# Windowed attention into a top-1 mixture of experts: the last routing groups, the row scale of the last two chunks and the early slices behind attention, put in another order and partly on another engine

## The chip, the cores and the metric

One core of one Trainium2 chip. The metric is the device time of one execution in microseconds (us), start to end. Engines: TensorE (PE, matmuls), VectorE (DVE), ScalarE (ACT), GpSimd (POOL), SyncE (SP, which here only issues DMA transfers). About 0.3% (2.0 us) is what a measurement of this kernel can tell from no change.

## The reference

Eight batches of eight heads, 576 positions of 64 numbers, causal attention in a window of 128 with a linear bias; then each of the 4,608 rows of 512 numbers goes to the one expert (of eight) with the largest logit.

```
scores = where(mask, q @ k.T / 8 + bias, -1e9)          # mask: 0 <= i - j < 128
attn = softmax(scores);  x = (attn @ v) as rows [4608, 512]
logits = x @ w_gate                                     # [4608, 8]
e = argmax(logits, 1);  g = softmax(logits)[e]
out[row] = g * (relu(x[row] @ w1[e]) @ w2[e])           # w1: 512x1024, w2: 1024x512
```

## The kernel before

**Attention** runs over 36 chunks of 128 rows, four steps for each, 152 steps in all. Through step 151 the order of every engine is the order in which the code is written. A chunk ends in `rows`: four pairs of matmuls (L206) form the 128 rows and their logits in the accumulation tile `r_ps`, of which there is one; VectorE takes the reciprocal of the softmax sum (L203) and multiplies by it (L211), first the 16 columns with the logits, then the 128 with the rows, into `x_sb`; `done` then sums the logits (`lg`, L1145) and issues the store of the rows to `xd` in HBM on SyncE's queue (L1152).

**Routing** (`route`, L404 to L470) runs over groups of chunks, `GROUPS`; a generator whose pieces are taken at the steps that `PACE` names. Its pieces: (a) `mx`, `sh`, `key`, `mk`, `oh`, `prev`: which expert each row has; (b) matmuls of `oh` with triangles (L421 to L425) in a tile borrowed from `r_ps` or from the early slices' tiles, and from it `pick`, the gates (`put_gates`, L488 to L496: the gate is written into a column of the same rows in `xd`, so its DMA must land behind the row's store), the running counts, `rank`, `t`; (c) `p`, `lp`, `c`, `big`; (d) `c`, `c`, `eq`, `rr`; (e) matmuls of `lp` with `rr` (L468), which are added to `base` (L470). `base` becomes the list of rows of each expert. The very last chunk, 35, has a short form, `route_last` (L500 to L553): its one-hot rows `l_oh`, its rank matmuls (L521), `l_rr`, four tiles `l_lp` (L542), eight small matmuls (L545), and `idx`, the list by which GpSimd gathers the rows of the first expert (`xg`, L589); the gather waits for all stores and gates.

**Early slices.** Expert 0's first 256 rows are known before attention ends. `moe_early` gathers them, transposes them in two tiles (matmuls at L598, `e_xh` on ScalarE, then `e_xl` on VectorE) and computes seven slices of the first layer on them, "0" to "6": twelve matmuls each (L637; the last four read `e_xl`), then `e_hh` on ScalarE (L640) and `e_hl` on VectorE (L641). `EP` names the steps of slices 0 to 2, and `LE` what `route_last` puts between its own parts ("3", "4", "5" and "6", nothing). `st["warm"](n)` runs entry n of `LE`, and each entry beyond the last slice lets matmuls of the second layer run: `y_ps` (L820), which need `e_hh` and `e_hl`; the first of them also needs the tile in which (e) of the last full group stood, so it waits for L470. Weights and inputs are split in a high and a low part, so every product is three matmuls.

The last full group before is that of chunks 30 to 34, its pieces (a) and (b) at steps 149 and 150 and the rest in `route_last`; the one ahead of it has chunks 27 to 29.

Of the kernel before, what the change touches and what calls it, by code (L numbers as in the profile page):

```python
# [36 lines left out]
def attention(ctx, tc, st, qT, kT, v, c1, cb, iw, load_c2, chunk_done, chunks, begun):  # L37
# [1081 lines left out]
def attn_moe_kernel(ctx, tc, qT, kT, v, c1, cb, c2, iw, w12, out):  # L1119
# [9 lines left out]
    with ExitStack() as actx:  # L1129
# [9 lines left out]
        def done(ch, subs, x_sb):  # L1139
# [7 lines left out]
            for lo in (0, 2):  # L1147
                if lo == 2 and subs[0][0] == subs[2][0]:
                    continue
                n = 64 if subs[0][0] != subs[2][0] else 128  # L1150
                t0 = subs[lo][0] * S + QB * subs[lo][1]
                nc.sync.dma_start(out=st["xd"][t0:t0 + n].rearrange("t (p x) -> t p x", p=NP),  # L1152
                                  in_=x_sb[QB * lo:QB * lo + n, :, 0:SUB])
# [67 lines left out]
```

## Time and profile before

| | |
|---|---|
| median of 3 runs | 672.38 us (671.96 to 673.99) |
| profiled execution | 670.84 us |
| its span | 669.1 us, so 1.7 us lie outside |
| PE / DVE / ACT / POOL busy | 645.0 / 397.8 / 315.3 / 311.7 us |

The change touches what runs between 217 and 256 us of the span: the end of attention, and the passage to the second layer of expert 0. Of each row of the trace one reads when an instruction began, how long it took, and, in square brackets, how long its engine had stood idle and what it then waited for. A row with a count stands for several instructions that follow each other.

### The profile page before, as it was taken

The page shows a single profiled execution, that of the slowest core. Times are in us where ns is not written, and L with a number is a line of the kernel's source. Part 1 is how long each engine was busy: PE and PEld are TensorE (multiplying, and loading weights), DVE is VectorE, ACT ScalarE, POOL GpSimd, SP SyncE. Part 2 cuts the span into 40 slices and gives each one's busy share as a digit, 9 for nine tenths or more (in the row PEclk, how much of TensorE's full clock was granted, in tenths as well). Part 3 has the DMA queues.
Part 4 walks back from the last instruction along what each step waited for, and adds up shares of the span by engine and source line. Part 5 has one row for each costly group of instructions (what it writes and reads, how often), then busy time and mean ns, then how long its engine had stood idle before and what let it go on. Part 6 is the DMA issues. An engine that isn't in the chain of part 4 may idle for free.

```text
span 669.1 us, 15750 instructions
## 1 busy us (share of the span) xinstructions
PE 645.0 (96%) x5985; PEld 546.8 (82%) x5985; DVE 397.8 (59%) x984; ACT 315.3 (47%) x957; POOL 311.7 (47%) x420
## 2 busy tenths in 40 slices
PE   8899999999999989999999999999999999999995
PEld 3587787887787878889888989898898989888884
DVE  3468878887888877554564465455456455456411
ACT  3677787888787521442343334233333333333311
POOL 2556466786764504016525742860762560471202
PEclk9999999999999999999999999999999999999998
DMA  8676797795862416428344433533542533454201
GB/s 316 200 199 175 182 235 174 241 260 151 259 160 65 97 50 190 126 111 273 106 146 151 132 100 110 163 101 97 168 125 84 183 105 82 157 145 110 91 1 58
DMA packets 57488, 98.43 MB, mean 147 GB/s; under 512 B 11701, under 2 KB 31413, under 8 KB 56514
## 3 DMA queue, kind: packets, MB, share of 16 engines
q1 hardware_dynamic: 48994, 77.38, 39.4%
q0 software_dynamic: 8416, 20.02, 10.5%
q8 instruction: 48, 0.79, 0.5%
q14 instruction: 30, 0.25, 0.1%
HBM read 78.40 MB, written 18.98 MB: 146 GB/s over the span
## 4 chain that ended last, share of the span: by engine, by line
PE 51%; issue 9%; POOL 4%; DVE 1%; DMA 1%; ACT 1%; POOLq 0%; ACTq 0%
PE y_ps L820 24%; PE l_ps L637 24%; POOL xg L617 2%; POOL out L808 1%; PE s_ps L637 1%; PE x_ps L598 1%; PE x_ps L196 1%; PE y_ps L780 1%; DMA xg<-xd,idx 0%; PE r_ps L206 0%; DMA xd<-x_sb 0%; DVE x_sb L211 0%; PE x_ps L780 0%; ACT pe L159 0%; POOLq L872 0%
## 5 line engine op out<-in xcount | busy, mean ns | idle before, releaser
L640 ACT ACTIVATE hh<-l_ps 128x336 fp32r<-128x336 f32 (+7 forms) x104 | 46.4, 447 | 203.4 <-PE l_ps L637 203.1
L641 DVE SCALAR_TENSOR_TENSOR hl<-l_ps,hh 128x336 fp32r<-128x336 f32 (+7 forms) x104 | 52.1, 502 | 150.2 <-ACT hh L640 150.1
L617 POOL DMA_INDIRECT xg<-xd,od_idx x112 | 118.1, 1054 | 36.9 <-issue 36.2
L159 ACT ACTIVATE pe<-s_ps,nmax 128x128 f32<-128x128 f32 x288 | 102.2, 371 | 48.9 <-DVE nmax L155 39.5
L820 PE MATMUL y_ps<-wh,hh 128*128 128x512 f32 (+5 forms) x280 | 110.9, 396 | 0.0
L820 PE MATMUL y_ps<-wh,hl 128*128 128x512 f32 (+5 forms) x280 | 110.4, 394 | 0.0
L820 PE MATMUL y_ps<-wl,hh 128*128 128x512 f32 (+5 forms) x280 | 110.3, 394 | 0.0
L808 POOL DMA_INDIRECT out<-y,od_pidx x33 | 34.8, 1055 | 149.3 <-ACT y L826 143.1
L912 DVE TENSOR_TENSOR wl<-w_raw,wh 128x512 fp32r<-128x512 f32 x114 | 73.8, 689 | 32.9 <-ACT wh L908 30.8
L637 PE MATMUL l_ps<-xh,wh 128*128 128x304 f32 (+9 forms) x416 | 81.7, 318 | 0.0
L637 PE MATMUL l_ps<-xh,wl 128*128 128x304 f32 (+9 forms) x416 | 81.0, 317 | 0.0
L637 PE MATMUL l_ps<-xl,wh 128*128 128x304 f32 (+9 forms) x416 | 80.8, 316 | 0.0
L637 PEld LDWEIGHTS l_ps<-xh,wh 128*128 128x128 f32 x416 | 68.1, 189 | 8.4 <-issue 1.2
L637 PEld LDWEIGHTS l_ps<-xh,wl 128*128 128x128 f32 x416 | 66.4, 189 | 1.9
L637 PEld LDWEIGHTS l_ps<-xl,wh 128*128 128x128 f32 x416 | 66.3, 189 | 1.7
L196 PE MATMUL x_ps<-pT,v_sb 128*64 128x128 f32 (+2 forms) x1152 | 66.3, 265 | 0.1
L196 PEld LDWEIGHTS x_ps<-pT,v_sb 128*64 128x64 f32 (+1 forms) x1152 | 57.0, 137 | 7.9 <-issue 2.8
L820 PEld LDWEIGHTS y_ps<-wh,hl 128*128 128x128 f32 (+5 forms) x280 | 51.4, 184 | 13.6
L908 ACT CAST wh<-w_raw 128x1024 fp32r<-128x1024 f32 x57 | 59.5, 1044 | 5.5 <-DMA w_raw<-w 5.5
L820 PEld LDWEIGHTS y_ps<-wl,hh 128*128 128x128 f32 (+5 forms) x280 | 51.6, 184 | 11.3
L159 ACT ACTIVATION_READ_ACCUMULATOR pe<-s_ps,nmax 128x1 f32 x288 | 60.2, 209 | 0.0
L138 PE MATMUL s_ps<-k_sb,q_sb 64*64 64x192 f32 (+2 forms) x1152 | 58.3, 311 | 1.9 <-DMA k_sb<-kT 1.9
(211 smaller groups left out, 972.6 us busy)
## 6 DMA issues: line engine op xcount, KB each, us to landing
w_raw<-w SPq DMA_DIRECT2D x64, 512.0 KB, 3.9
q_sb<-qT SPq DMA_DIRECT2D x40, 256.0 KB, 6.4
xd<-x_sb SPq DMA_DIRECT2D x32, 258.0 KB, 4.8
v_sb<-v SPq DMA_DIRECT2D x32, 256.0 KB, 5.2
k_sb<-kT SPq DMA_DIRECT2D x7, 1152.0 KB, 8.5
w_n<-w SPq DMA_DIRECT2D x4, 1024.0 KB, 8.0
xg<-xd,od_idx POOLq DMA_INDIRECT x112, 2.9
xd<-x_sb SPq DMA_DIRECT2D x8, 129.0 KB, 4.8
```

What stands on the lines that cost most here:

```text
L138: nc.tensor.matmul(out=s_ps[halves(a), c, n, x0:x1], lhsT=blocks["q", b, m][h, 2 * g + n, qs], rhs=batch[b][h, 2 * g + n, k0:k0 + x1 - x0] ...
L159: nc.scalar.activation(out=pe[:, h, :], in_=s_ps[:, c, n, lo:lo + 128], func=AF.Exp, bias=nmax[:, 2 * c + n:2 * c + n + 1], scale=1.0, acc ...
L196: nc.tensor.matmul(out=x_ps[64 * c:64 * c + 64, p, q], lhsT=blocks["v", b, m - 1 + kb][0:kk, D * h:D * h + D], rhs=pT[0:kk, kb, h, q], sta ...
L598: nc.tensor.transpose(out=x_ps[:, d, :], in_=g[:, SUB * d:SUB * d + 128], identity=st["ident"])
L617: ins = tc.nc.gpsimd.indirect_dma_start(out=g[:, s], out_offset=None, in_=parts, in_offset=bass.IndirectOffsetOnAxis(ap=idx[:, s], axis=0),)
L637: nc.tensor.matmul(out=ps, lhsT=a[:, 128 * d:128 * d + 128], rhs=b[:, d], start=(k == 0), stop=(k == 11))
L640: nc.scalar.activation(out=hh, in_=ps, func=AF.Relu)
L641: nc.vector.scalar_tensor_tensor(out=hl, in0=ps, scalar=0.0, in1=hh.bitcast(F32), op0=ALU.max, op1=ALU.subtract)
L808: ins = nc.gpsimd.indirect_dma_start(**kw).ins
L820: nc.tensor.matmul(out=ys[t][0:n], lhsT=a[:, tl], rhs=b[:, 512:1024], start=(f == 0 and k == 0), stop=(f == 7 and k == 2))
L908: keep(tc, nc.scalar.copy(out=wh, in_=raw))
L912: keep(tc, eng.tensor_tensor(out=wl[:, sl], in0=raw[:, sl], in1=wh.bitcast(F32)[:, sl], op=ALU.subtract))
```

## The change

- The last full groups are cut anew: chunks 27 to 31 (five), then 32 to 34 (three). The pieces of the five are at steps 142, 144, 145, 146 and 148, in place of those of 27 to 29 at 138, 142, 144, 146 and 148. Pieces (a) and (b) of the three are at steps 149 and 150.
- In the last full group the cuts between the pieces lie elsewhere: `t`, `p`, `lp` are one piece, taken ahead of slices 5 and 6; gates, `c`, `big`, `c`, `c`, `eq`, `rr` are the next one, taken behind slices 5 and 6. The first half of its `rr` goes to GpSimd.
- For chunks 34 and 35 the long half of the row scale (128 columns) is no longer one operation of VectorE but eight of ScalarE, one for each head, each with its column of `rinv` as scale. They and the row's store are put off: for 34 behind the piece of step 149, for 35 behind `l_pick` in `route_last`.
- Slices 1 and 2 stand at step 149 one behind the other, each in a tile of its own; before, 2 was at step 150, behind the rank matmuls of the group. In `route_last` slice 3 has its matmuls where they were, and its `e_hh` and `e_hl` stand behind `l_pick`.
- The four `l_lp` are made ahead of slice 4, and the eight matmuls that use them (L545 before) stand in a row ahead of the first matmul of the second layer, not among those.

```
-PACE = {21: (122, 126, 130, 132, 134), 27: (138, 142, 144, 146, 148), 30: (149, 150)}
-GROUPS = ((0, 5), (5, 5), (10, 5), (15, 6), (21, 6), (27, 3), (30, 5), (35, 1))
+PACE = {21: (122, 126, 130, 132, 134), 27: (142, 144, 145, 146, 148), 32: (149, 150)}
+GROUPS = ((0, 5), (5, 5), (10, 5), (15, 6), (21, 6), (27, 5), (32, 3), (35, 1))
...
-EP = {60: "z", 134: "g", 143: "p0", 146: "p1", 147: "0", 149: "1", 150: "2"}
+EP = {60: ("z",), 134: ("g",), 143: ("p0",), 146: ("p1",), 147: "0", 149: "12"}
...
+        def scale_heads():
+            for h in range(H):
+                cols = slice(D * (h % 2), D * (h % 2) + D)
+                nc.scalar.activation(out=x_sb[:, h // 2, cols], in_=r_ps[:, h // 2, cols], func=AF.Copy, scale=rinv[:, h:h + 1])
+
+        scale(128, E)
+        if ch < N // 128 - 2:
+            scale(0, D)
+        chunk_done(ch, subs, x_sb, scale_heads)
...
+    final = c0 + G == N // 128 - 1
...
+    if final:
+        yield
+        gates()
     c = rp.tile([128, G], F32, name="c")
...
-        nc.vector.tensor_tensor(out=rr[:, :, k, :], in0=eq,
+        eng = nc.gpsimd if final and k == 0 else nc.vector
+        eng.tensor_tensor(out=rr[:, :, k, :], in0=eq,
...
+    for evict in st.pop("later"):
+        evict()
+    st.pop("store")()
     put_gates(tc, st, gate, groups)
-    st["warm"](2)
+    t0 = EARLY // 128
+    lps = {}
+    for t in range(t0, TT):
+        lps[t] = rp.tile([128, 128], BF16, name=f"l_lp{t}", bufs=1)
+        nc.vector.tensor_scalar(out=lps[t], in0=st["i128"], scalar1=s, scalar2=-128.0 * t, op0=ALU.subtract,
+                                op1=ALU.is_equal)
+    for n in (1, 2, 3):
+        st["warm"](n)
+        for r in st["rest"]:
+            if n < 3:
+                next(r)
     for r in st["rest"]:
         list(r)
...
-    st["warm"](3)
...
+            if ch < N // 128 - 2:
+                store()
+            else:
+                st["store"] = lambda: (scale(), store())
```

Of what moves, three places. First VectorE between the two `e_xl`, near the end of attention. Before, piece (b) of the group of three is over when the first `e_xl` comes, and (c) and (d) stand around the `x_sb` of chunk 32 (line numbers are those of each kernel):

```order
L438 TENSOR_SCALAR t<-t 128x3
L601 TENSOR_TENSOR e_xl<-s_ps,e_xh 128x4x128
L602 COPY e_gate<-e_xg 128x1
L446 SCALAR_TENSOR_TENSOR p<-t,rank 128x3
L448 TENSOR_TENSOR lp<-c_sb,p 128x384
L451 TENSOR_SCALAR c<-mk 128x3
L453 TENSOR_SCALAR big<-rank 128x3
L203 RECIPROCAL rinv<-rsum 128x8
L211 TENSOR_TENSOR x_sb<-r_ps,rinv 128x4x16
L211 TENSOR_TENSOR x_sb<-r_ps,rinv 128x4x128
L1145 TENSOR_REDUCE lg<-x_sb 128x8
L455 TENSOR_TENSOR c<-c,t 128x3
```

and now piece (b) of the group of five stands behind the first `e_xl`, ahead of that `x_sb`,

```order
L632 TENSOR_TENSOR e_xl<-s_ps,e_xh 128x4x128
L633 COPY e_gate<-e_xg 128x1
L439 TENSOR_TENSOR pick<-r_ps,oh 128x40
L444 TENSOR_REDUCE gate<-ex 128x5
L517 TENSOR_SCALAR gate<-gate 128x5
L519 RECIPROCAL gate_4279<-gate 128x5
L450 TENSOR_REDUCE run<-oh 128x8
L451 TENSOR_TENSOR run<-run 128x8
L453 TENSOR_REDUCE rank<-pick 128x5
L457 TENSOR_SCALAR t<-rank 128x5
L458 TENSOR_SCALAR t<-t 128x5
L203 RECIPROCAL rinv<-rsum 128x8
```

with (c) and (d) of the five in one piece ahead of the second `e_xl`:

```order
L467 SCALAR_TENSOR_TENSOR p<-t,rank 128x5
L469 TENSOR_TENSOR lp<-c_sb,p 128x640
L475 TENSOR_SCALAR c<-mk 128x5
L477 TENSOR_SCALAR big<-rank 128x5
L480 TENSOR_TENSOR c<-c,t 128x5
L481 TENSOR_TENSOR c<-c,big 128x5
L483 TENSOR_TENSOR eq<-c_sb,c 128x240
L488 TENSOR_TENSOR rr<-eq,c_sb 128x5x48 x2
L632 TENSOR_TENSOR e_xl<-s_ps,e_xh 128x4x128
```

So `pick`, which frees the `r_ps` that the matmuls of chunk 32 take, moved behind `e_xl`, and the second `e_xl` behind the whole of a longer block.

Second, VectorE from the `e_hl` of slice 5 on. Before, (c) and (d) of the last full group are over by then, and only `base` follows the last `e_hl`:

```order
L641 SCALAR_TENSOR_TENSOR e_hl<-s_ps,e_hh 128x256
L529 TENSOR_SCALAR l_rr<-l_oh,c_sb 128x8 x2
L532 ISA l_pick,rank<-x_ps,l_oh 128x8
L532 ISA rank 128x1
L491 TENSOR_SCALAR l_gate<-l_gate 128x1
L493 RECIPROCAL gate_4574<-l_gate 128x1
L641 SCALAR_TENSOR_TENSOR e_hl<-s_ps,e_hh 128x256 x2
L470 TENSOR_TENSOR base<-base,t_ps 128x48
```

Now the two `e_hl` of slices 5 and 6 come first, and gates, `c`, `big`, `eq` and VectorE's half of `rr` stand between them and `base`:

```order
L674 SCALAR_TENSOR_TENSOR e_hl<-s_ps,e_hh 128x256 x2
L444 TENSOR_REDUCE gate<-ex 128x3
L517 TENSOR_SCALAR gate<-gate 128x3
L519 RECIPROCAL gate_4623<-gate 128x3
L475 TENSOR_SCALAR c<-mk 128x3
L477 TENSOR_SCALAR big<-rank 128x3
L480 TENSOR_TENSOR c<-c,t 128x3
L481 TENSOR_TENSOR c<-c,big 128x3
L483 TENSOR_TENSOR eq<-c_sb,c 128x144
L488 TENSOR_TENSOR rr<-eq,c_sb 128x3x48
L496 TENSOR_TENSOR base<-base,t_ps 128x48
```

Nine operations moved behind the last slice; the four `l_lp` that stood behind `base` are gone from there.

Third, ScalarE between the `e_hh` of slice 0 and that of slice 6. Before:

```order
L640 ACTIVATE e_hh<-s_ps 128x256
L239 COPY xT<-x_ps 128x512
L411 ACTIVATE ex<-sh 128x40
L640 ACTIVATE e_hh<-s_ps 128x256 x2
L515 ACTIVATE l_ex,l_gate<-lg,l_mx 128x8
L640 ACTIVATE e_hh<-s_ps 128x256
L1033 COPY sel<-c_sb 128x512
L640 ACTIVATE e_hh<-s_ps 128x256 x3
```

Now, with the eight scales of chunk 34 ahead of the `e_hh` of slices 1 and 2, and those of chunk 35 between the ones of slices 3 and 4:

```order
L673 ACTIVATE e_hh<-s_ps 128x256
L249 COPY xT<-x_ps 128x512
L423 ACTIVATE ex<-sh 128x24
L219 ACTIVATE x_sb<-r_ps,rinv 128x64 x8
L673 ACTIVATE e_hh<-s_ps 128x256 x2
L541 ACTIVATE l_ex,l_gate<-lg,l_mx 128x8
L673 ACTIVATE e_hh<-s_ps 128x256
L219 ACTIVATE x_sb<-r_ps,rinv 128x64 x8
L673 ACTIVATE e_hh<-s_ps 128x256
L1068 COPY sel<-c_sb 128x512
L673 ACTIVATE e_hh<-s_ps 128x256 x2
```

The `e_hh` of slices 1 and 2 moved behind eight scales, that of slice 4 behind another eight.

## Rows read from the trace of the kernel before

**Rows 1.** The view that cuts the span into stretches, around the passage to the second layer: start and end of the stretch and its length, busy time of each engine with its instructions in brackets, granted clock of TensorE, share of the DMA engines, GB/s.

```profile
238.00:244.00 6.00, 4.98 (x45) 4.87 (x45) 4.93 (x27) 1.67 (x6) 0.00 (x0) 1.00 0.23 49
244.00:250.00 6.00, 4.56 (x44) 4.22 (x42) 4.54 (x21) 1.19 (x4) 0.00 (x0) 1.00 0.17 46
250.00:256.00 6.00, 5.81 (x33) 4.12 (x33) 3.75 (x28) 0.22 (x1) 2.86 (x3) 1.00 0.34 89
256.00:292.00 36.00, 36.00 (x232) 31.72 (x231) 23.11 (x66) 13.78 (x31) 6.03 (x6) 1.00 0.53 169
```

**Rows 2.** The timeline of TensorE's matmuls from 222 to 256 us: start, duration, engine, line, operation, out<-in, shape, count, and in square brackets the idle time ahead of it with what ended it.

```profile
225.63 1.15 PE L206 MATMUL r_ps<-iw_sb,xT 128*128 128x144 f32 x8
227.22 0.65 PE L168 MATMUL t_ps<-c_sb,pe 128*128 128x128 f32 x4 [0.44 <-ACT pT L170]
...
232.80 1.97 PE L196 MATMUL x_ps<-pT,v_sb 128*64 128x128 f32 x32
...
238.36 0.18 PE L421 MATMUL t_ps<-oh,tri 128*128 128x40 bf16 x1 [0.84 <-DVE oh L415]
...
240.07 1.14 PE L206 MATMUL r_ps<-iw_sb,xT 128*128 128x144 f32 x8
...
243.29 0.17 PE L521 MATMUL x_ps<-l_oh,tri 128*128 128x8 bf16 x1 [0.66 <-DVE l_oh L517]
...
247.00 0.75 PE L637 MATMUL s_ps<-e_xh,wh 128*128 128x256 f32 x4 [0.57 <-DVE e_hl L641]
...
248.55 0.42 PE L468 MATMUL t_ps<-rr,lp 128*128 128x48 bf16 x10
249.84 0.47 PE L820 MATMUL y_ps<-wh,e_hh 128*128 128x512 f32 x1 [0.87 <-DVE base L470]
...
251.34 0.39 PE L820 MATMUL y_ps<-wl,e_hh 128*128 128x512 f32 x1
...
255.04 0.66 PE L598 MATMUL x_ps<-c_sb,xg 128*128 128x128 f32 x4 [0.19 <-DMA xg<-xd,idx]
```

**Rows 3.** The timeline of VectorE over the same place, columns as in the group ahead.

```profile
226.72 0.69 DVE L601 TENSOR_TENSOR e_xl<-s_ps,e_xh 128x512 fp32r<-128x512 f32 x1 [1.17 <-ACT e_xh L600]
...
227.38 0.50 DVE L446 SCALAR_TENSOR_TENSOR p<-t,rank 128x3 f32<-128x3 f32 x1
227.92 0.56 DVE L448 TENSOR_TENSOR lp<-c_sb,p 128x384 bf16<-128x384 f32 x1
228.40 0.60 DVE L451 TENSOR_SCALAR c<-mk 128x3 f32<-128x3 f32 x1
...
231.34 0.68 DVE L601 TENSOR_TENSOR e_xl<-s_ps,e_xh 128x512 fp32r<-128x512 f32 x1
...
238.75 0.20 DVE L427 TENSOR_TENSOR pick<-t_ps,oh 128x40 f32<-128x40 f32 x1
...
240.12 0.17 DVE L438 TENSOR_SCALAR t<-t 128x5 f32<-128x5 f32 x1
...
241.31 0.82 DVE L211 TENSOR_TENSOR x_sb<-r_ps,rinv 128x64 f32<-128x64 f32 x2
...
243.00 0.23 DVE L517 TENSOR_SCALAR l_oh<-l_key,mk 128x8 bf16<-128x8 f32 x1
...
243.90 0.16 DVE L446 SCALAR_TENSOR_TENSOR p<-t,rank 128x5 f32<-128x5 f32 x1
...
244.84 0.17 DVE L451 TENSOR_SCALAR c<-mk 128x5 f32<-128x5 f32 x1
...
245.88 0.73 DVE L462 TENSOR_TENSOR rr<-eq,c_sb 128x240 bf16<-128x240 f32 x2
...
249.50 0.19 DVE L470 TENSOR_TENSOR base<-base,t_ps 128x48 f32<-128x48 f32 x1
```

**Rows 4.** The timeline of GpSimd there (L589 is the issue of the gather that L598 of TensorE waits for), and the form of its longer elementwise operation (the view by line and shape: count, then busy time in all and mean ns of one).

```profile
227.24 0.63 POOL L178 TENSOR_SCALAR_AFFINE_SELECT pT<-pT 128x512 f32<-128x512 f32 x1 [1.24 <-ACT pT L170]
227.94 1.03 POOL L180 TENSOR_SCALAR_AFFINE_SELECT pT<-pT 128x512 f32<-128x512 f32 x1
...
251.69 0.96 POOL L589 DMA_INDIRECT xg<-xd,idx  x1 [21.42 <-DVE base L550]
...
L929 POOL TENSOR_TENSOR wl<-w_raw,wh 128x512 fp32r<-128x512 f32 x14 | 18.4, 1316 | 3.5 <-ACT wh L924 3.3
```

**Rows 5.** The view by line and shape for ScalarE: two sizes of the operation that multiplies by a column of scales; then its timeline, with two operations that follow each other without a pause.

```profile
L826 ACT ACTIVATE y<-y_ps,e_gate 128x512 f32<-128x512 f32 x2 | 1.4, 687 | 1.0 <-PE y_ps L820 1.0
...
L790 ACT ACTIVATE y<-x_ps,g_n 128x128 f32<-128x128 f32 x1 | 0.4, 369 | 0.4 <-PE x_ps L780 0.4
...
225.60 0.60 ACT L239 COPY xT<-x_ps 128x512 f32<-128x512 f32 x1
226.06 0.62 ACT L600 CAST e_xh<-s_ps 128x512 fp32r<-128x512 f32 x1
```

**Rows 6.** The issues on the queue of SyncE there, and the median time from issue to landing of such transfers between 220 and 256 us (KB of all of them, then us).

```profile
243.12 0.54 SPq L1152 DMA_DIRECT2D xd<-x_sb  x1
247.58 0.33 SPq L496 DMA_DIRECT2D xd<-gate  x1
...
xd<-x_sb SPq DMA_DIRECT2D x4, 258.0 KB, 3.7
...
xd<-gate SPq DMA_DIRECT2D x2, 1.5 KB, 2.8
```

More of the change, by code (lines that the diff above doesn't have):

```diff
@@ L207, in rows, with scale @@
         x_sb = xp.tile([128, NP, XW], F32, name="x_sb")
-        for lo, n in ((128, E), (0, D)):
+        def scale(lo, n):
             cols = slice(lo, lo + 2 * n)
@@ L285, in step @@
                     st["stages"].remove(k)
+        if "store" in st:
+            st.pop("store")()
         n, i = divmod(s - FETCH, 8)
@@ L290, in step @@
             st["load"]((s - FETCH + 12) // 8)
-        if s in EP:
-            early(EP[s])
+        for op in EP.get(s, ()):
+            early(op)
     with tc.manual_schedule(engines=HANDS(nc)):
@@ L427, in route, with gates @@
     nc.vector.tensor_tensor(out=pick, in0=rank.rearrange("p (g e) -> p g e", e=E), in1=oh, op=ALU.mult)
-    gate = rp.tile([128, G], F32, name="gate")
-    nc.vector.tensor_reduce(out=gate, in_=ex, axis=AX.X, op=ALU.add)
-    put_gates(tc, st, gate, groups)
+    final = c0 + G == N // 128 - 1
+    def gates():
+        gate = rp.tile([128, G], F32, name="gate")
+        nc.vector.tensor_reduce(out=gate, in_=ex, axis=AX.X, op=ALU.add)
+        put_gates(tc, st, gate, groups)
+    if not final:
+        gates()
     new = run[:, c0 + G, :]
@@ L441, in route @@
         nc.vector.tensor_copy(out=cnt, in_=new)
-    yield
+    if not final:
+        yield
     if c0 + G == LATE:
@@ L449, in route @@
                             in1=p.unsqueeze(2).to_broadcast(sp3), op=ALU.is_equal)
+    if final:
+        yield
+        gates()
     c = rp.tile([128, G], F32, name="c")
@@ L517, in route_last @@
     nc.vector.tensor_scalar(out=oh, in0=key, scalar1=mk, scalar2=None, op0=ALU.is_equal)
+    st["later"] = []
     st["warm"](0)
@@ L538, in route_last @@
     ip = st["ps_x"].tile([128, 512], F32, name="x_ps")[:, 0:E * TT]
-    t0 = EARLY // 128
     for t in range(t0, TT):
-        lp = rp.tile([128, 128], BF16, name=f"l_lp{t}", bufs=1)
-        nc.vector.tensor_scalar(out=lp, in0=st["i128"], scalar1=s, scalar2=-128.0 * t, op0=ALU.subtract,
-                                op1=ALU.is_equal)
         for k in range(2):
-            nc.tensor.matmul(out=ip[:, E * t:E * t + E], lhsT=lp, rhs=rr[:, k, :], start=(k == 0), stop=(k == 1))
+            nc.tensor.matmul(out=ip[:, E * t:E * t + E], lhsT=lps[t], rhs=rr[:, k, :], start=(k == 0), stop=(k == 1))
     v = lambda ap: ap.rearrange("p (e t) -> p t e", t=TT)
@@ L639, in first_layer, with evict @@
     ps = ps[:, 0:hh.shape[1]]
-    nc.scalar.activation(out=hh, in_=ps, func=AF.Relu)
-    nc.vector.scalar_tensor_tensor(out=hl, in0=ps, scalar=0.0, in1=hh.bitcast(F32), op0=ALU.max, op1=ALU.subtract)
+    def evict():
+        nc.scalar.activation(out=hh, in_=ps, func=AF.Relu)
+        nc.vector.scalar_tensor_tensor(out=hl, in0=ps, scalar=0.0, in1=hh.bitcast(F32), op0=ALU.max, op1=ALU.subtract)
+    evict() if later is None else later.append(evict)
 def moe_early(ctx, tc, st):
@@ L1137, in begun, with done @@
                     keep(tc, nc.vector.tensor_copy(out=st["hl"][:, :, j], in_=st[n]))
-        def done(ch, subs, x_sb):
+        def done(ch, subs, x_sb, scale):
             c0, G = next((c, n) for c, n in GROUPS if c <= ch < c + n)
@@ L1146, in done, with store @@
                                     axis=AX.XY, op=ALU.add)
[L1147 to L1153, printed above, removed]
+            def store():
+                for lo in (0, 2):
+                    if lo == 2 and subs[0][0] == subs[2][0]:
+                        continue
+                    n = 64 if subs[0][0] != subs[2][0] else 128
+                    t0 = subs[lo][0] * S + QB * subs[lo][1]
+                    nc.sync.dma_start(out=st["xd"][t0:t0 + n].rearrange("t (p x) -> t p x", p=NP),
+                                      in_=x_sb[QB * lo:QB * lo + n, :, 0:SUB])
+            if ch < N // 128 - 2:
+                store()
+            else:
+                st["store"] = lambda: (scale(), store())
             if g == G - 1:
```

13 lines of the change are left out of this document (5 added, 8 removed).

## The prediction

> **What bounds the kernel now.** I read the stretches first, then TensorE's timeline, and then, wait by wait, the engine that ended it. TensorE bounds the kernel: from 256 to 292 us it is busy for all 36.00 of 36.00 us, while from 238 to 256 it stands idle for 1.02, 1.44 and 0.19 us of three times six [rows 1]. So the change can only work on TensorE's idle time around this place, and whatever moves the matmul that first uses rows gathered behind routing (L598 at 255.04) moves the end as much, since nothing behind it has air to take a shift up. The reader is to see six waits [rows 2]: 0.44 us ahead of the transposes at 227.22, 0.84 ahead of the last group's rank matmuls, 0.66 ahead of the last chunk's, 0.57 ahead of slice 6, 0.87 ahead of the second layer, 0.19 for the gather; 3.57 us in all. Four of the six end on VectorE. That is the most that could be had there, and every operation that VectorE gets at the wrong place costs as much. I go along TensorE in order and carry the shift against before. A shift here is one of the span; outside the span 1.7 us stay as they are.
>
> **1. The group of five ahead of slice 0.** Before, the row matmuls of chunk 32 start at 225.63 [rows 2]. They need `r_ps`, in which the rank of the group stands until `pick` has read it, and `pick` of the five now stands behind the first `e_xl`, which runs 226.72 to 227.41 since it waits for ScalarE, as before [rows 3]. So `pick` ends at about 227.6 and the row matmuls start 2.0 us later than before. The 0.44 wait behind them and 0.15 of drain are swallowed: the shift on TensorE's side is +1.4. On VectorE's side the five's piece (b) is 1.54 us (238.75 to 240.12 + 0.17), the `x_sb` of chunk 32 with its sums takes to about 230.1, and (c) with (d) of a group of five is 2.7 us (243.90 to 245.88 + 0.73) [rows 3]: the second `e_xl` begins at 232.8 instead of 231.34, +1.46. The last matmuls of slice 0 need it, so both sides agree: the attention matmuls at 232.80 come **+1.4**.
>
> **2. What GpSimd adds to that.** The trace shows one block (c) beside GpSimd at work on `pT`: `p` took 0.50 and `c` 0.60 us, against 0.16 and 0.17 with GpSimd idle [rows 3], so 0.34 + 0.43 = 0.77. `p` ended at 227.88 as GpSimd's operation ended at 227.87; `c` ended at 229.00 as the next one ended at 228.97, and that one took 1.03 instead of 0.63 while VectorE's `lp` ran [rows 3, 4]. The last two operations on `pT` move back by the same 1.4 us as the transposes ahead of them, to about 230.3 to 231.7, and the five's `p` and `c` begin at 230.1 and 231.0. I take the 0.77 in full; the bounds are 0 (no meeting) and 1.0 (three small operations meet). **+0.77**, in all +2.2 at 232.80.
>
> **3. Slices 1 and 2 together, long scale on ScalarE.** With slice 2 behind slice 1 the last group's rank is no longer waited for: **-0.84**; the rank of three has two matmuls less, at most 0.1. So the row matmuls of chunk 35 come at 240.07 + 1.3. From the `x_sb` of chunk 35 to the end of `l_oh` it is 241.31 to 243.23 = 1.92 us, and the long half that is dropped is about 0.60 of it. But two `e_hl` and `pick` to `rank` now stand ahead, and the `e_hl` wait for `e_hh` behind the eight scales of chunk 34. No scale of 128x64 is in the trace; a scale by a column takes 0.369 us at 128x128 and 0.687 at 128x512, which a line carries to 0.32 at 64, and neighbours on ScalarE overlap by 0.14 (225.60 + 0.60 against 226.06) [rows 5]. So eight take 8 x 0.18 + 0.14 = 1.6, bounds 1.0 (0.13 each) and 2.1 (0.27 each). They start at about 238.7 without GpSimd's share, the two `e_hh` end at 241.0, the `e_hl` at 241.5, `pick` to `rank` at 242.1, and 0.14 + 1.32 later `l_oh`, so the last rank matmul comes at 243.6 instead of 243.29. A wait of about 0.8 us stands where 0.66 stood: **+0.33** here, +1.1 with step 2. In "ScalarE: Activation LUTs", section "What ACT_TABLE_LOAD costs", the Trainium skill gives an ACTIVATE 186 ns + 0.833 ns an element, some 93 ns more for a column operand and 93 ns of overlap: by that a scale is an estimated 0.24 us and eight are 2.0, and this step and the sum would be 0.4 us more; no row of before has the shape.
>
> **4. Slice 6.** Its wait of 0.57 goes, because `e_hl` of slice 4 no longer stands behind a block (c), (d); four `l_lp` and `p`, `lp` of three fit in. Slice 6: +0.33 - 0.57 = **-0.24** against 247.00, +0.5 with step 2.
>
> **5. The last group's end.** Before, (d) was done at 246.61, so the `lp` matmuls followed slice 6 at 248.55 without a wait, and `base` began behind the last `e_hl` at 249.50 [rows 2, 3]. Now VectorE begins there, at 249.50 - 0.24 = 249.26, with the gates (three operations, about 0.5), `c`, `big`, `c`, `c` (0.6) and `eq` (0.34), to 250.7. What covers such a block elsewhere, a slice's matmuls, is used up: `LE` has nothing left behind slice 6. Then `rr`: 0.31 us on VectorE; on GpSimd 128x512 took 1.316 [rows 4], so 128x144 is 0.37 by elements, 0.5 with a start of 0.2. Whether the halves run side by side the trace does not show for `rr`; step 2's rows show VectorE and GpSimd taking turns. So `rr` is over at 250.7 + 0.31 + 0.5 = 251.5, or 251.2 if they overlap. The "SBUF — State Buffer" page of the Trainium skill, section "SBUF: two separate sides", says that the two engines share a pair of ports as an exclusive lock, which an operation of VectorE with two inputs there holds against GpSimd to its end, and the reverse; that speaks against the split, and the rows of step 2 agree with it. Then six matmuls (0.36, as the ten took 0.42) and `base` to the first `y_ps` (249.50 to 249.84, 0.34): 252.2 against 249.84. **+2.36**, +3.1 with step 2.
>
> **6. Back among the second layer.** The eight `l_lp` matmuls and their waits no longer stand between the first `y_ps`: the first four took 249.84 to 251.34 = 1.50, four without them about 0.97 (the later 14 took 3.51, with one more small matmul). The 0.19 goes too if the gather is there. **-0.72.**
>
> Is it there? `idx` waits for nothing more, so the gather can start 0.45 behind the first `y_ps`, at 252.7 (253.4 with step 2), and L598 may follow 3.35 later, as before (251.69 to 255.04) [rows 2, 4]: 0.6 earlier than it would come. It also needs the gates. The scales of chunk 35 end at 245.5, the store follows (before at 243.12, landing 3.7 later [rows 6]) and lands at 249.3, then a gate issue of 0.33, then the group's three columns, 2.8 to landing: 252.4, and 0.4 to GpSimd: 252.8; with step 2, 253.6. A tie within 0.2; I count nothing, and the price is in the second rival.
>
> Edits that I cost at nothing: slice 3's put-off `e_hh` has a tile of its own and ends 2 us before its use; the five's gate DMAs at 229 to 232 stand ahead of stores that no one reads until the gather; the removed pieces of 27 to 29 at 217 to 225 lie beside full matmuls.
>
> **Sum.** 1.4 - 0.94 - 0.13 (step 3 to +0.33) - 0.57 + 2.60 - 0.72 = +1.64, and 0.77 for GpSimd: **+2.4 us**. 670.84 becomes 673.2; the median of 672.38 becomes **674.8** (+0.36%).
>
> **The rivals.** *GpSimd stays out* (0.35): step 2 is nothing or half, or the halves of `rr` overlap: +1.1 to +2.0, 673.5 to 674.4, within what can be told from no change. For it: only two operations of the block were hit before; against: the block falls on the very time. *The gates end last* (0.11): the chain rank, scales of 35, store, gate, three gates is longer than `base`; it decides when the scales cost over 0.24 or a store over 4.0; then L598 waits 0.5 to 1.0: 675.3 to 675.8. *Faster* (0.05): the changed order does on VectorE what it is laid out for. That needs `rr` of the three done when slice 6 ends, and `r_ps` free by 226.0; then steps 1, 2 and 5 are nothing, -0.84, -0.57, -0.72 stay, with +0.2 of step 3: 670.5. Against it stands the order itself, nine operations behind the last `e_hl`; it decides at whether the wait ahead of the last group's `lp` matmuls is under 0.3 us. *The clock* (0.04): in all stretches above 1.00 was granted [rows 1], that is the 2.4 GHz level; TensorE will do only 14 small matmuls in 4 us, and if the grant falls to the lower level, matmuls of 4 us take 2 us more: 676.8. *No doing together* (0.03): if slice 2 still waits for a tile, 0.84 stays: 675.6.
>
> **How the numbers follow.** My forecast has 0.42, with 674.4 to 675.3. The range leaves out what is faster and the low end of the first rival below, the clock above: 673.0 to 676.2. About 0.3% (2.0 us) is what a measurement can tell, so slower begins at 674.4: forecast, gates, clock and no doing together give 0.60; same 0.35; faster 0.05.
>
> **What would show it.** Right: the row matmuls of chunk 32 wait for `pick`, near 227.6; slice 0's last matmuls wait for `e_xl`; no wait between slices 1 and 2; a wait of 0.8 at the last rank; none ahead of slice 6; one of about 3 us, the longest, behind slice 6, ended by `rr` of GpSimd or VectorE; `y_ps` in steps of 0.23. Wrong: scales over 0.25 each; a wait at L598 for the gather; `p` and `c` of the five at 0.17; a clock under 1.00 near 250.

## The result, and the profile after

The changed kernel takes 676.31 us (median of 5, 675.11 to 678.27) against 672.38: the medians lie 3.9 us apart, and the ratio is 1.0063, 95% interval [1.0049, 1.0077], so it is slower. The profiled execution took 676.2 us, span 674.5. The direction and the waits were as forecast; the time lies outside the range of 673.0 to 676.2, because a fall of TensorE's clock came on top, which the sum had at nothing.

The places of the argument stand in these views of the changed kernel (its line numbers; L855 is L820 of before, L629 is L598). First the stretches, to be held against [rows 1]; the second column is the length, then the busy times, then the granted clock:

```profile
244.00:250.00 6.00, 5.07 (x43) 4.84 (x42) 4.38 (x25) 3.85 (x15) 0.00 (x0) 1.00 0.17 49
250.00:256.00 6.00, 3.38 (x22) 2.71 (x22) 2.93 (x19) 0.00 (x0) 2.40 (x3) 0.82 0.14 14
256.00:262.00 6.00, 6.00 (x30) 4.55 (x28) 3.83 (x22) 0.59 (x1) 1.03 (x2) 0.89 0.40 124
```

TensorE's timeline, to be held against [rows 2]:

```profile
228.01 1.25 PE L206 MATMUL r_ps<-iw_sb,xT 128*128 128x144 f32 x8 [1.98 <-DVE pick L439]
...
234.68 0.73 PE L668 MATMUL s_ps<-e_xl,wh 128*128 128x256 f32 x4 [0.57 <-DVE e_gate L633]
235.34 1.97 PE L196 MATMUL x_ps<-pT,v_sb 128*64 128x128 f32 x32
...
241.81 1.25 PE L206 MATMUL r_ps<-iw_sb,xT 128*128 128x144 f32 x8
...
245.00 0.17 PE L548 MATMUL x_ps<-l_oh,tri 128*128 128x8 bf16 x1 [0.50 <-DVE l_oh L543]
...
247.98 0.64 PE L668 MATMUL s_ps<-e_xh,wh 128*128 128x256 f32 x4
...
252.41 0.31 PE L494 MATMUL t_ps<-rr,lp 128*128 128x48 bf16 x6 [2.85 <-POOL rr L488]
...
253.11 0.47 PE L855 MATMUL y_ps<-wh,e_hh 128*128 128x512 f32 x1 [0.20 <-DVE base L496]
253.42 0.40 PE L855 MATMUL y_ps<-wl,e_hh 128*128 128x512 f32 x1
...
254.32 0.63 PE L855 MATMUL y_ps<-wl,e_hh 128*128 128x512 f32 x1
254.75 0.63 PE L855 MATMUL y_ps<-wh,e_hl 128*128 128x512 f32 x1
...
259.05 0.60 PE L629 MATMUL x_ps<-c_sb,xg 128*128 128x128 f32 x4
```

VectorE's, to be held against [rows 3]:

```profile
227.77 0.19 DVE L439 TENSOR_TENSOR pick<-r_ps,oh 128x40 f32<-128x40 f32 x1
...
230.61 0.43 DVE L467 SCALAR_TENSOR_TENSOR p<-t,rank 128x5 f32<-128x5 f32 x1
...
231.81 0.60 DVE L475 TENSOR_SCALAR c<-mk 128x5 f32<-128x5 f32 x1
...
250.02 0.43 DVE L674 SCALAR_TENSOR_TENSOR e_hl<-s_ps,e_hh 128x256 fp32r<-128x256 f32 x1 [1.00 <-ACT e_hh L673]
250.36 0.17 DVE L444 TENSOR_REDUCE gate<-ex 128x3 f32<-128x24 f32 x1
...
251.43 0.31 DVE L483 TENSOR_TENSOR eq<-c_sb,c 128x144 f32<-128x144 f32 x1
251.77 0.31 DVE L488 TENSOR_TENSOR rr<-eq,c_sb 128x144 bf16<-128x144 f32 x1
```

GpSimd's and ScalarE's:

```profile
231.09 1.30 POOL L180 TENSOR_SCALAR_AFFINE_SELECT pT<-pT 128x512 f32<-128x512 f32 x1
251.82 0.54 POOL L488 TENSOR_TENSOR rr<-eq,c_sb 128x144 bf16<-128x144 f32 x1 [19.43 <-DVE eq L483]
...
253.84 0.99 POOL L620 DMA_INDIRECT xg<-xd,idx  x1 [1.48 <-DVE od_base L1094]
```

```profile
240.01 1.75 ACT L219 ACTIVATE x_sb<-r_ps,rinv 128x64 f32<-128x64 f32 x8
...
245.14 1.74 ACT L219 ACTIVATE x_sb<-r_ps,rinv 128x64 f32<-128x64 f32 x8
```

What one is to see. The row matmuls of chunk 32 wait 1.98 us for `pick`; slice 0's last matmuls wait 0.57 for the second `e_xl` (the row names `e_gate`, the next operation behind it); the waits ahead of the last group's rank and of slice 6 are gone; 2.85 us are lost behind slice 6, where VectorE goes from the last `e_hl` at 250.02 through the gates (from 250.36) to `eq` and `rr`. All this the prediction has, save that the wait at the last rank is 0.50 us and not 0.8. What it gave a chance of 0.04: behind those 2.85 us the second layer's matmuls, 0.23 us apart at first, come 0.43 us apart from 253.9 to 257.3, and the stretch from 250 to 256 has a granted clock of 0.82, the next one 0.89.

Executions begin attention a little earlier or later, so I count from the start of the last matmul of scores (L138; 222.23 before, 222.49 after), which the change leaves alone. Each entry is the start of a matmul less that start, in us; the last column is the distance from the first `y_ps` to L598:

| kernel | rows 32 | slice 0, last four | rows 35 | last rank | slice 6 | first y_ps | L598 | y_ps to L598 |
|---|---|---|---|---|---|---|---|---|
| before | 3.40 | 10.00 | 17.84 | 21.06 | 24.77 | 27.61 | 32.81 | 5.20 |
| changed | 5.52 | 12.19 | 19.32 | 22.51 | 25.49 | 30.62 | 36.56 | 5.94 |
| e4_fill | 5.53 | 13.07 | 20.12 | 23.30 | 26.28 | 31.40 | 36.12 | 4.71 |
| e5_fill_both | 5.53 | 12.19 | 19.34 | 22.52 | 25.50 | 30.62 | 34.98 | 4.36 |
| e1_block_ahead | 5.52 | 13.07 | 20.12 | 23.30 | 26.28 | 29.64 | 35.44 | 5.79 |
| e2_block_store | 5.52 | 12.19 | 19.35 | 22.52 | 25.62 | 29.14 | 33.60 | 4.46 |
| e7_scale34_dve | 5.52 | 12.19 | 19.09 | 22.23 | 25.31 | 28.83 | 33.45 | 4.62 |
| e3_old_cut | 3.40 | 10.00 | 16.97 | 20.73 | 23.83 | 27.62 | 33.54 | 5.92 |
| b1_lp_ahead | 3.28 | 10.00 | 17.84 | 21.06 | 24.77 | 27.60 | 31.94 | 4.35 |
| b2_lp_12_scale35 | 3.41 | 10.01 | 16.72 | 20.74 | 25.27 | 28.09 | 32.43 | 4.33 |
| e10_block_behind | 3.41 | 9.99 | 17.82 | 21.04 | 24.02 | 30.06 | 37.25 | 7.19 |
| e9_rr_dve | 5.52 | 12.19 | 19.34 | 22.52 | 25.49 | 30.52 | 34.86 | 4.34 |
| e8_best | 3.40 | 10.00 | 16.71 | 20.33 | 23.42 | 27.16 | 31.51 | 4.35 |

The changed kernel's L598 is 3.75 us later. Of the 5.12 by which its last matmul is later (667.02 against 661.90), 0.26 are that attention ended later, and 1.1 come behind L598, in single waits that are not the change's: from L598 to the last matmul it is 406.86 us before and 407.97 changed, but 408.84 in `b1_lp_ahead`, which is faster than before, and 406.88 in `e10_block_behind`, which is slower than the changed kernel.

### The profile page after: what moved, and what is told of

It reads as the page before. It is cut to its first block, busy times and chain, and to the rows that moved or that the text cites. A ratio compares the mean times of both kernels' runs of the same rounds, so it can differ in the third digit from the quotient of the medians.

```text
span 674.5 us, 15760 instructions
## 1 busy us (share of the span) xinstructions
PE 645.2 (96%) x5983; PEld 546.9 (81%) x5985; DVE 395.5 (59%) x981; ACT 317.3 (47%) x973; POOL 309.9 (46%) x421
## 4 chain that ended last, share of the span: by engine, by line
PE 52%; issue 10%; POOL 2%; ACT 1%; DVE 1%; POOLq 0%; another core or an unknown queue 0%; ACTq 0%; DVEq 0%
PE y_ps L855 26%; PE l_ps L668 25%; POOL out L843 1%; POOL xg L648 1%; PE x_ps L629 1%; PE y_ps L815 1%; ACT pe L159 0%; PE x_ps L815 0%; DVE s_ps L152 0%; DVE nmax L155 0%; POOL pT L180 0%; POOLq L907 0%; PE r_ps L206 0%; PE t_ps L168 0%
## 5 line engine op out<-in xcount | busy, mean ns | idle before, releaser
L648 POOL DMA_INDIRECT xg<-xd,od_idx x112 | 115.8, 1034 | 36.6 <-issue 36.3
L855 PE MATMUL y_ps<-wh,hh 128*128 128x512 f32 (+5 forms) x280 | 110.9, 396 | 0.1
L855 PE MATMUL y_ps<-wh,hl 128*128 128x512 f32 (+5 forms) x280 | 110.4, 394 | 0.0
L855 PE MATMUL y_ps<-wl,hh 128*128 128x512 f32 (+5 forms) x280 | 110.2, 394 | 0.0
L855 PEld LDWEIGHTS y_ps<-wh,hl 128*128 128x128 f32 (+5 forms) x280 | 51.3, 183 | 13.7 <-DVE hl L674 0.2
L855 PEld LDWEIGHTS y_ps<-wl,hh 128*128 128x128 f32 (+5 forms) x280 | 51.5, 184 | 11.4
L855 PEld LDWEIGHTS y_ps<-wh,hh 128*128 128x128 f32 (+5 forms) x280 | 51.4, 183 | 10.7 <-ACT hh L673 0.7
```

Of the source, the lines that this page charges most:

```text
L648: ins = tc.nc.gpsimd.indirect_dma_start(out=g[:, s], out_offset=None, in_=parts, in_offset=bass.IndirectOffsetOnAxis(ap=idx[:, s], axis=0),)
L855: nc.tensor.matmul(out=ys[t][0:n], lhsT=a[:, tl], rhs=b[:, 512:1024], start=(f == 0 and k == 0), stop=(f == 7 and k == 2))
```

## The experiments

All comparisons are ratios to the kernel before on the same chip (its median was 672.41 us in the first set of four, 669.30 and 669.22 in the later ones). A ratio is not the quotient of the two medians given with it; the two differ by up to about 0.001, so a difference of some tenths of a us between runs says nothing.

**e4_fill**, the changed kernel with nine matmuls on zeros behind slice 6:

```
-LW = (0, 0, 0, 0)
+LW = (0, 0, 9, 0)
```

> The changed kernel with nine idle matmuls of 128x512 (about 0.23 us each, 2.1 us in all) laid into the 2.9 us in which TensorE waits for the last group's pieces behind slice 6; nothing else is changed. Theory A: the granted clock falls at 253.9 us because TensorE stood idle just ahead of it, and the nine second-layer matmuls at the lower level cost 1.5 us. Then no stretch here is under 1.00, the first 18 second-layer matmuls come 0.23 us apart, and the time is 1.5 us below the changed kernel's 676.3: 674.8. Rival B: the fall has another cause (what TensorE did over the 20 us ahead, or the second layer itself): clock near 0.8 as before, 676.3.

675.20 against 672.41, ratio 1.0036 [1.0023, 1.0049]. The clock stays at 1.00 from 250 us on; `y_ps` to L598 is 4.71 instead of 5.94. So the fall did come from the pause: `e5_fill_both` and `e9_rr_dve`, with the same nine matmuls, have none there either. (It is 4.36 in `e5_fill_both`; the other 0.35 us are a later gather, not slow matmuls: here it begins 1.35 us behind the first `y_ps`, there 0.67.) The same trace shows another fall that I hadn't expected, at chunk 34's attention matmuls, behind the 1.98 wait for `pick`:

```profile
227.78 1.25 PE L206 MATMUL r_ps<-iw_sb,xT 128*128 128x144 f32 x8 [1.98 <-DVE pick L439]
...
229.60 3.38 PE L196 MATMUL x_ps<-pT,v_sb 128*64 128x128 f32 x32
...
252.96 0.31 PE L494 MATMUL t_ps<-rr,lp 128*128 128x48 bf16 x6 [0.89 <-POOL rr L488]
```

```profile
228.00:229.00 1.00, 1.00 (x10) 1.00 (x10) 0.90 (x6) 0.00 (x0) 0.67 (x2) 1.00 0.00 0
229.00:230.00 1.00, 1.00 (x9) 0.67 (x9) 0.88 (x5) 0.29 (x1) 0.00 (x0) 0.56 0.28 2
230.00:231.00 1.00, 1.00 (x14) 1.00 (x12) 0.96 (x4) 0.29 (x1) 0.64 (x1) 0.50 0.05 0
231.00:232.00 1.00, 1.00 (x12) 1.00 (x10) 1.00 (x2) 0.00 (x0) 0.93 (x2) 0.50 0.50 143
...
253.00:256.00 3.00, 2.79 (x24) 2.33 (x24) 1.04 (x9) 0.00 (x0) 0.99 (x1) 1.00 0.06 0
```

The 32 matmuls take 3.38 us, 1.97 at the full clock; 0.88 of it is left at slice 0's last four (13.07 against 12.19), since `e_xl` is waited for there anyhow.

**e1_block_ahead**, the changed kernel with the last group's block ahead of slices 5 and 6:

```
-LE = ("3", "4", "56", "")
+LE = ("3", "4", "", "56")
```

> The changed kernel with the last group's gates, c, big, eq and rr taken ahead of slices 5 and 6, not behind them. Theory A: the wait behind slice 6 shrinks from 2.85 to about 1.1 us, no fall of the clock follows; but the gates, which land behind chunk 35's store, then end last: the first matmul on gathered rows waits 1 to 1.5 us for them and comes about 1.9 us earlier than in the changed kernel: 674.4. Rival B (the clock falls anyway): 676. Rival C (the gather is not held by the gates): 3.3 us earlier, 673.0.

675.66, ratio 1.0044 [1.0030, 1.0059]: more than expected. Its profile has the fall at chunk 34 again (0.88), none behind slice 6, where 1.08 us are lost instead of 2.85; and L598 waits for the gather:

```profile
252.32 0.31 PE L494 MATMUL t_ps<-rr,lp 128*128 128x48 bf16 x6 [1.08 <-DVE e_hl L674]
...
258.81 0.66 PE L629 MATMUL x_ps<-c_sb,xg 128*128 128x128 f32 x4 [1.29 <-DMA xg<-xd,idx]
```

Without the early fall its L598 would be 2.0 us ahead of the changed kernel's, as theory A has it; in the time, 0.6 us (medians) or 1.3 (ratios) of that is seen, and the two intervals overlap.

**e2_block_store**, e1 and the scales and store of chunk 35 ahead of `l_prev`:

```
+    st.pop("store")()
     prev = rp.tile([128, E], BF16, name="l_prev", bufs=1)
...
-    st.pop("store")()
     put_gates(tc, st, gate, groups)
```

> As the run with the block ahead of slices 5 and 6, and the eight scales and the store of chunk 35 are issued at once behind its row matmuls, some 2 us earlier. Theory A: the store lands 2 us earlier, the gates no longer end last, and the first matmul on gathered rows comes 3.3 us earlier than in the changed kernel: 673.0 (within 1 us of before, since the shift ahead of slice 0 stays). Rival C (the store and the gates were not the bound): no difference to the run ahead of it.

673.75, ratio 1.0014 [1.0002, 1.0025]. L598 waits for nothing and comes 2.96 us earlier than in the changed kernel. So in e1 the store and the gates behind it were the bound, and rival C falls. The trace of e2 has no early fall either, which is some 0.88 of the 1.84 us between e1's L598 and its own.

**b1_lp_ahead**, the kernel before with term 6 alone:

```
+    t0 = EARLY // 128
+    lps = {}
+    for t in range(t0, TT):
+        lps[t] = ...
     st["warm"](2)
...
-            nc.tensor.matmul(out=ip[:, E * t:E * t + E], lhsT=lp, ...
+            nc.tensor.matmul(out=ip[:, E * t:E * t + E], lhsT=lps[t], ...
```

> The kernel before with one part of the change alone: the four l_lp are made ahead of slices 5 and 6, and the eight matmuls that use them stand ahead of the second layer instead of among it. Theory A, term 6 of the prediction: first matmul on gathered rows 0.72 us earlier, 671.7. Rival: the gather or the four l_lp ahead of the e_hl of slices 5 and 6 take it back: 672.4.

671.20, ratio 0.9983 [0.9970, 0.9996]: faster than before by its interval, though by less than the 0.3% named at the start. First `y_ps` where it was (27.60), L598 0.87 earlier; the term was 0.72.

**e5_fill_both**, e4 and six more matmuls on zeros behind the rank matmuls of the five.

```
-LW = (0, 0, 0, 0)
+LW = (0, 0, 9, 0, 6)
...
+    if c0 == 27:
+        st["warm"](4)
     pick = rp.tile(sh3, F32, name="pick")
```

> The run with nine idle matmuls behind slice 6, and six more laid into the 2.0 us in which TensorE waits for pick ahead of chunk 32's row matmuls. Theory A, now widened: the clock falls behind each of the two long waits, behind the first one only in some executions (in that run's profile the attention matmuls of chunk 34 took 3.38 us instead of 1.97, at a granted clock of 0.50). Then no stretch is under 1.00, the executions lie closer together, and the median is 0.4 to 0.8 us lower: 674.4 to 674.8. Rival: the fall at chunk 34 has to do with something else than the wait: 675.2 with falls in half of the executions.

671.21 against 669.30, ratio 1.0040 [1.0025, 1.0055]. By the medians that is 1.9 us above before, where e4 was 2.8 above; by the ratios there is no gain over e4. Six executions don't decide between the two, so the median part of that expectation stays open; its other part missed, since the executions lie no closer together (670.67 to 673.19, e4 674.35 to 676.49). No stretch near the change is under 1.00:

```profile
250.00:253.00 3.00, 2.80 (x24) 2.30 (x20) 1.04 (x9) 0.00 (x0) 1.53 (x2) 1.00 0.08 12
253.00:256.00 3.00, 3.00 (x17) 2.29 (x16) 2.26 (x16) 0.46 (x1) 1.35 (x2) 1.00 0.72 190
```

```profile
250.50 0.47 PE L857 MATMUL y_ps<-wh,e_hh 128*128 128x512 f32 x1 [0.20 <-DVE base L498]
...
254.86 0.60 PE L631 MATMUL x_ps<-c_sb,xg 128*128 128x128 f32 x4
```

Of the six profiles with the 1.98 wait unfilled, two have an early fall (e1, e4) and four have none (changed, e2, e7, e9); the filled one has none either. Each run also lists the mean granted clock of every execution; one fall like that of the changed kernel (half the clock from 253.9 to 257.3, of 674.5 us) lowers it by an estimated 0.0025. Against before on the same chip the mean over all executions is 0.0011 lower in e4 (0.9953 against 0.9964) and 0.0037 lower in e7 (0.9931 against 0.9968), and 0.0009 higher here (0.9977 against 0.9968). So the executions of e7 lose more clock than its profile shows; where in them is not known, so the share of the early fall in the medians stays open. The trace of e5 is the change without any fall: L598 (L631 here) at 34.98, **2.17 us** later than before.

**e10_block_behind**, the kernel before with its last group's block alone moved behind slice 6:

```
-    for r in st["rest"]:
-        next(r)
-        next(r)
     st["warm"](1)
```

> The kernel before with one thing alone moved: p, lp, c, big, eq, rr of its last group (2.7 us of VectorE) stand behind the e_hl of slices 5 and 6. Theory A: the 0.57 wait of slice 6 goes, a wait of about 3.6 us comes behind slice 6, 2.5 us are lost by that, and the clock falls behind it as in the changed kernel, 1.4 us more: 3.9 us slower than before. Rival: the fall in the changed kernel needs something else of the change (its first wait, GpSimd): 2.5 us slower with the clock at 1.00.

673.76 against 669.22, ratio 1.0072 [1.0052, 1.0091]: this one move costs 4.5 us, no less than the whole change (the intervals overlap). L817 and L595 are L820 and L598 of before.

```profile
249.36 0.83 PE L468 MATMUL t_ps<-rr,lp 128*128 128x48 bf16 x10 [3.23 <-DVE rr L462]
...
253.28 0.63 PE L817 MATMUL y_ps<-wl,e_hh 128*128 128x512 f32 x1
253.71 0.63 PE L817 MATMUL y_ps<-wh,e_hl 128*128 128x512 f32 x1
...
256.02 0.39 PE L817 MATMUL y_ps<-wh,e_hl 128*128 128x512 f32 x1
...
257.77 0.60 PE L595 MATMUL x_ps<-c_sb,xg 128*128 128x128 f32 x4
```

```profile
247.00:250.00 3.00, 0.55 (x10) 0.45 (x10) 2.49 (x10) 0.00 (x0) 0.00 (x0) 0.82 0.00 0
250.00:253.00 3.00, 2.61 (x17) 1.59 (x15) 1.10 (x6) 0.00 (x0) 0.00 (x0) 0.50 0.00 0
253.00:256.00 3.00, 3.00 (x8) 2.35 (x8) 0.74 (x8) 0.00 (x0) 2.01 (x3) 0.54 0.29 73
256.00:260.00 4.00, 4.00 (x21) 2.97 (x19) 3.34 (x19) 0.59 (x1) 0.85 (x1) 1.00 0.49 143
```

The wait is 3.23 us, and the clock is at 0.50 from 250 to 253. Distance from `y_ps` to L598: 7.19 against 5.20, so the fall takes 2.0 us here, and the first `y_ps` is 2.45 later. So neither GpSimd nor the first wait is needed for the fall.

**e3_old_cut**, e2 with the groups cut as before and the last group's gates with its rank:

```
-PACE = {21: (122, 126, 130, 132, 134), 27: (142, 144, 145, 146, 148), 32: (149, 150)}
+PACE = {21: (122, 126, 130, 132, 134), 27: (138, 142, 144, 146, 148), 30: (149, 150)}
...
-    if not final:
-        gates()
+    gates()
```

> The run with the block and the store ahead, and the groups cut as before the change (27 to 29, then 30 to 34, the gates of the last one taken with its rank as before). Theory A: what that run still loses against before, 0.9 us, is the five's pieces ahead of slice 0; without them chunk 32's row matmuls wait for nothing, no fall of the clock there, and the first matmul on gathered rows comes 0.9 us earlier than in the kernel before: 671.5. Rival: the cut costs nothing, the loss is the long scale on ScalarE: 673.7.

669.44 against 669.30, ratio 1.0001 [0.9990, 1.0012]. Chunk 32 and slice 0 are back at 3.40 and 10.00. But the clock falls here too, behind waits of 1.08 us (last rank) and 1.42 (`rr`):

```profile
244.00:250.00 6.00, 4.38 (x45) 3.95 (x44) 4.86 (x24) 0.77 (x2) 1.73 (x2) 0.97 0.12 31
250.00:253.00 3.00, 3.00 (x9) 2.02 (x8) 0.00 (x0) 0.00 (x0) 1.96 (x3) 0.50 0.56 147
```

So `y_ps` to L598 is 5.92, and the 0.9 us that were expected are given back by the clock; without it, L598 would be at about 32.0 (an estimate, with the 4.36 of e5). That these two waits brought the fall is not shown: in `b2_lp_12_scale35` waits of 1.37 and 1.24 us, 4.5 us apart, brought none.

**e7_scale34_dve**, e2 with chunk 34's long scale and store as before:

```
-        if ch < N // 128 - 2:
+        if ch < N // 128 - 1:
             scale(0, D)
```

> The run with the block and the store ahead, with the long scale of chunk 34 back on VectorE and only chunk 35's on ScalarE. Theory A: the eight scales of chunk 34 hold up the e_hh and e_hl of slices 1 and 2, which stand ahead of the last chunk's x_sb, so without them l_oh comes 0.4 us earlier: 673.3. Rival: VectorE has no room for the 0.6 us: 674.3.

671.01 against 669.30, ratio 1.0030 [1.0018, 1.0043]. The trace has what theory A says, the last rank 0.29 earlier than in e2, but little of it is left at L598 (33.45 against 33.60), and the time, from another chip than e2's, doesn't show it. What spreads the time goes with the clock: the three executions with a mean granted clock of 0.997 or more, the profiled one among them, took 669.5 to 669.9 us, the five with 0.990 or 0.991 took 670.8 to 672.3. Inconclusive.

**b2_lp_12_scale35**, b1 with slices 1 and 2 back to back and chunk 35's long scale on ScalarE, ahead of its store.

```
-EP = {..., 147: "0", 149: "1", 150: "2"}
+EP = {..., 147: "0", 149: "12"}
...
+        if ch == 35:
+            for h in range(H):
+                nc.scalar.activation(out=x_sb[...], in_=r_ps[...], func=AF.Copy, scale=rinv[:, h:h + 1])
```

> The kernel before with the l_lp ahead (671.2 measured), slices 1 and 2 back to back, and the long scale of chunk 35 alone on ScalarE, at once. Theory A: the 0.84 wait ahead of the last group's rank goes, VectorE's pick to t then come 0.4 later, the 0.6 saved at x_sb makes that good: the last rank matmul 0.3 to 0.4 us earlier, 670.8. Rival: the wait only moves to the last rank matmul: 671.2.

668.32 against 669.30, ratio 0.9991 [0.9979, 1.0002]: no gain over b1, where one was expected. The last rank comes 0.32 earlier, as expected, but then slice 6 waits for `e_hl` of slice 4, behind the five's block:

```profile
240.97 0.17 PE L525 MATMUL x_ps<-l_oh,tri 128*128 128x8 bf16 x1 [1.37 <-DVE l_oh L521]
...
245.50 0.75 PE L643 MATMUL s_ps<-e_xh,wh 128*128 128x256 f32 x4 [1.24 <-DVE e_hl L647]
```

1.24 us instead of 0.57: the 0.84 taken from one wait went to two others (the last rank's was 0.66, slice 6's 0.57), and L598 is 0.5 later than in b1.

**e9_rr_dve**, e4 with both halves of `rr` on VectorE:

```
-        eng = nc.gpsimd if final and k == 0 else nc.vector
+        eng = nc.vector
```

> The run with nine idle matmuls behind slice 6, and both halves of the last group's rr on VectorE. If the halves ran side by side before (VectorE's ended 0.3 us ahead of GpSimd's in the changed kernel's trace), rr ends within 0.05 us of where it did and the ratio to before stays at 1.0036. If GpSimd's half had been held up by VectorE's, 0.2 to 0.3 us are won.

671.50 against 669.22, ratio 1.0032 [1.0021, 1.0043]: the split moves nothing that can be measured.

```profile
249.61 0.31 DVE L483 TENSOR_TENSOR eq<-c_sb,c 128x144 f32<-128x144 f32 x1
249.95 0.53 DVE L488 TENSOR_TENSOR rr<-eq,c_sb 128x144 bf16<-128x144 f32 x2
```

From the start of `eq` to the end of `rr` it is 0.87 us here; split, it is 0.93 (251.43 to 251.82 + 0.54). That is no sign that the halves ran side by side; step 5 below looks at that.

**e8_best**, e3 with chunk 34's scale and `rr` on VectorE, and `LW = (0, 0, 0, 4)`:

> The run with the old cut of the groups, with the long scale on ScalarE for chunk 35 only, rr on VectorE alone, and four idle matmuls ahead of the last group's lp matmuls. Theory A: without the fall of the clock that the old cut's run still had (1.5 us) and with 0.4 us less of waiting, the first matmul on gathered rows comes 1.2 to 1.3 us earlier than in the kernel before, ratio 0.998, about as the run with the l_lp ahead alone (0.9983). Rival: the clock falls in spite of the idle matmuls: 1.000.

667.90 against 669.22, ratio 0.9982 [0.9971, 0.9994], clock 1.00 around the change, L598 at 31.51, 1.30 earlier than before. By its interval it beats both kernels, though before by less than 0.3%, and by no more than b1 does with far less of an edit.

## Why the prediction was right and where it was wrong

**Steps 1 and 2** (+2.17 at slice 0's last four): measured +2.19. `p` and `c` of the five took 0.43 and 0.60, and GpSimd's operation beside them 1.30 instead of 0.63; 0.77 was taken in full, 0.27 + 0.43 = 0.70 came.

**Step 3** (+1.1 at the last rank): +1.45. The eight scales took 1.75 us, not 1.6 (and 1.74 for chunk 35). The figure of the Trainium skill ("ScalarE: Activation LUTs", section "What ACT_TABLE_LOAD costs") led to 2.0, so the trace lies between the two. The rest: the scales began 0.3 us later than forecast, and from the end of `rank` (243.29) to the end of `l_oh` (244.94) it took 1.65, not 1.46; what lies between took a little less than forecast.

**Step 4** (+0.5 at slice 6): +0.72, the 0.57 gone.

**Step 5** (+3.1 at the first `y_ps`): +3.01. The wait is 2.85, its size near the 3 us named. One piece of it was off: from the end of `eq` to the end of `rr` it is 0.62 us, where 0.31 + 0.5 stood. VectorE's half ran 251.77 to 252.08 and GpSimd's 251.82 to 252.36. The two overlap in the rows, but VectorE's began first, so its undisturbed 0.31 says nothing of GpSimd's. Elsewhere in this trace GpSimd is seen to wait for such an `rr`: its small sum `rsum` (128x8, L263) takes 0.20 us in 28 of 36 places, and in the four where VectorE was at an `rr` it took 0.22 to 0.49 and ended 0.06 behind the end of that `rr` (the other four stand beside the operation of L147). So GpSimd's half most likely waited too, and then took 0.28 where the forecast had 0.5: by that the halves were rightly counted one after the other, and GpSimd's own part was 0.2 too large. The rule of the Trainium skill ("SBUF — State Buffer", section "SBUF: two separate sides") fits `p`, `c` and `lp` and these rows of `rsum`.

**Step 6** (-0.72): -0.84 in the e5 run, -0.87 in b1; in the changed kernel itself +0.74. **This is the step that failed**: it took the second layer at 0.23 us a matmul, though step 5 had just put a pause of 3 us ahead of it; the fall of the clock behind that pause stood in the sum at nothing. The clock stood among the rivals, with 2.0 us, and got 0.04. It cost 5.94 - 4.36 = 1.58 us. The ground given was that every stretch shown had 1.00; but the trace of before has no such pause (from 10 us on no wait of TensorE in it is over 1.17 us), so the rows could say nothing against it. Nor did a row give the 4 us of slow matmuls that the rival's price was made of.

The sum without the clock was +2.4; measured without it (e5 against before) +2.17. Part of that closeness is luck: up to the last rank the forecast was 0.35 short, and behind it 0.6 too long. 2.17 + 1.58 is the 3.75 at L598, and the medians' 3.9 leaves 0.2 for the early fall in some executions and for chance. The gates did not end last: the gather started 0.73 behind the first `y_ps` (253.84), within the tie that was named, and L598 found the rows there. It did so without slow matmuls too: in e5 the gather starts 0.67 behind the first `y_ps`, and L598 waits for nothing. In e1, where the first `y_ps` comes 0.98 earlier, it waited 1.29.

## What to carry to other kernels

Where an edit opens a pause on a TensorE that was kept busy, the pause is not the whole price: look whether the granted clock falls behind it, and give the fall a price and a real chance even where no row has it yet; here it cost 1.58 us behind a pause of 2.85, and 2.0 behind one of 3.23. A few matmuls on zeros in the pause tell the two prices apart, and here gave back most of the second one. A wait on the path that is removed only pays if the next wait on the same engine isn't sized by the same work: 0.84 us taken from the rank came back at the last rank and at slice 6, while the plain move of eight small matmuls and their tiles out of the second layer paid in full.

## What the runs showed of the hardware

With waits of 2.85 and 3.23 us TensorE's clock fell to the lower of its two levels (0.50 granted) in both traces that have them; behind one of 1.98 us in two traces of six; behind 1.08 and 1.42 us some 6 us apart in one (`e3_old_cut`); not behind 1.24 us in `e2_block_store`, and not behind 1.37 and 1.24 us in `b2_lp_12_scale35`. Equal waits thus had a fall in one trace and none in another. In the changed kernel it was low from 253.9 to 257.3, beginning 1.5 us behind the end of the pause, where matmuls ran again; in `e10_block_behind` from 248.9 to 255.8, beginning within the pause. With nine matmuls in the 2.85 us it didn't fall there, in three traces of three. The "TensorE: Matmul & The Clock Gate" page of the Trainium skill, section "What's actually happening", has a gate that goes by how busy TensorE has lately been, and these rows agree with it.
